# Four buffers take their places in SBUF ahead of the 3456-byte buffer, in a one-core fp32 block of attention and Mish MLP

## The chip, the cores and the metric

The kernel runs on one core of one Trainium2 chip. The metric is the device time of one execution in microseconds; lower is better. Three runs of the kernel before took 1113.59, 1114.18 and 1112.23 us, the median is 1113.59 us. A further execution was recorded by the profiler and took 1110.76 us.

## What is computed

The reference takes x of 2048 tokens by 576 features, normalises it, and adds two branches to it:

```python
def reference(A_x, A_wqkv, A_wo, B_x, B_w1, B_b1, B_w2):
    x = A_x
    xn = _layernorm(x, axis=-1)
    return x + _A_ref(xn, A_wqkv, A_wo) + _B_ref(xn, B_w1, B_b1, B_w2)

def _A_ref(x, wqkv, wo):         # 32 heads of 18; each token sees 8 tokens, 2 apart, backwards
    ...
    logits = jnp.einsum("bhsd,bhswd->bhsw", q, kg) * scale
    logits = jnp.where(mask[None, None, :, :], logits, -1e9)
    attn = _softmax(logits, axis=-1)
    o = jnp.einsum("bhsw,bhswd->bhsd", attn, vg)
    return (lambda x, *d: x.transpose(*d))(o, 0, 2, 1, 3).reshape(B, S, D) @ wo

def _B_ref(x, w1, b1, w2):       # 576 -> 4608 -> 576
    h = jnp.einsum("bsd,df->bsf", x, w1) + b1
    sp = jnp.log1p(jnp.exp(-jnp.abs(h))) + jnp.where(h > 0, h, jnp.zeros_like(h))
    act = h * jnp.tanh(sp)
    return jnp.einsum("bsf,fd->bsd", act, w2)
```

## The kernel before

**Numbers.** Every matrix product runs on TensorE in a rounded fp32 type. To keep fp32 accuracy each operand is split into a high and a low part, and three products (high by high, high by low, low by high) are summed in PSUM. A weight tile therefore holds two halves: `t[:, 0]` is the high part (a ScalarE copy, line 365) and `t[:, 1]` the low part (a VectorE subtraction, line 366).

**Tiling.** The tokens go in two halves `hf` of 1024, each in two blocks `b` of 512 tokens. The transposed, normalised input of a block is the tile `xt` (one for each block, `X0` and `X1` in the code); sums of the two blocks are the tiles `S`. The 4608 hidden features go in 18 pairs `q` of 128-column blocks. The products of the MLP are done with seven products of half blocks where eight would be usual, so the weights of a pair appear in four tiles: `wa` (the first weight block as it is, 640 columns), `wc` (a part of the second, 384 columns) and `t0`, `t1` (differences, 512 columns each).

**The first product** of the MLP is `m1_part` (lines 892 to 925). For each `hf` and `q` it runs six parts. `prod` (line 830) issues six matmuls, each with a 128x128 piece of a weight tile held in TensorE and 512 columns of `xt` or `S` streamed past it; `rest` (line 838) issues two more for the last 64 features. Part 0 is 14 matmuls with `wa` against `X0` (12 from line 834, 2 from line 840), and part 4 ends with 2 matmuls with `wa` against `X1` (line 840). So `wa` is the held weight in 16 matmuls of each of the 36 steps. All the other parts hold pieces of `t0`, `t1` or `wc`.

**The second product** (`m2_pair` line 927, `m2_cols` line 1042, `p_item` line 1016) holds a piece of an activation tile (`act` or `u`) and streams 288 columns of the second weight.

**Order.** The instructions stand in an order written by hand: a list `plan` of steps, to which the code attaches small functions (loads, splits, attention steps) by tables of offsets. Each engine executes its own list in that order and waits on semaphores where it needs another engine. SyncE's queue carries every load and store. Attention runs beside the products: GpSimd multiplies (lines 697 and 736), VectorE reduces (702, 742), VectorE transposes the result `og` of a pair of heads groups into `oT` (line 762), and four or more stores write `oT` to DRAM (line 771).

**Places in SBUF.** Tiles are requested from one pool by a tag. A tag gets its place the first time that it is requested, behind the places given before, and all later tiles of the tag use it again. The last ones to be given are these, in bytes from the start of a partition, as the built program has them:

| tile (tag) | first byte before | size |
|---|---|---|
| 3456-byte buffer (`r3`) | 206,400 | 3456 |
| `wa` of even q (`wa1`) | 209,856 | 5120 |
| `q`, two buffers | 214,976 and 216,128 | 1152 each |
| `wa` of odd q (`wa0`) | 217,280 | 5120 |
| `L`, two buffers | 222,400 and 223,424 | 1024 each |
| `m`, two buffers | 224,448 and 224,576 | 128 each |
| `og` | 224,704 | 2304 |
| `oT` | 227,008 | 2304 |

The 3456-byte buffer is requested first by `za_high` (line 515) for a weight tile of the query, key and value projection, by way of the table `YHOME` (line 495, `"T2": ("r3", "a0")`). It serves later as a place for other weights and for one raw activation. All other weight and input tiles lie below it: `wq`, `t0`, `t1` at 60,224, 64,320 and 68,416; `xt` of the two blocks at 85,312 and 161,344; `wc` at 103,744 and 107,328; the second weights at 110,912 to 124,736; activations at 140,864 to 157,248; `S` at 181,824, 190,016 and 198,208.

Of the kernel before, what the change touches and what calls it, by code (L numbers as in the profile page):

```python
# [9 lines left out]
F32 = mybir.dt.float32  # L10
F32R = mybir.dt.float32r
# [7 lines left out]
P = 128  # L19
# [4 lines left out]
TJ = SH // P  # L24
# [6 lines left out]
PU = 2  # L31
CU = 2 * DH
# [98 lines left out]
def block_kernel(ctx: ExitStack, tc: tile.TileContext, x, wq, wo, w1, b1, w2, mask, out):  # L131
# [4 lines left out]
    sb = ctx.enter_context(tc.tile_pool(name="sb", bufs=2))  # L136
# [97 lines left out]
    def newton1():  # L234
        newton(rs1, ve1, y1, nc.gpsimd)
        nc.gpsimd.tensor_mul(nm1, mv1[:, :, 0:1], rs1)
        nc.gpsimd.tensor_scalar(nm1, nm1, -1.0, None, op0=ALU.mult)
# [74 lines left out]
    def home(kind, i):  # L312
        if kind == "wq":
            g, k = divmod(i, 5)
            tag, bufs = (("wb", 3) if k < 3 else ("wc", 2)) if g % 2 == 0 else (("a0", 3) if k < 3 else ("a1", 2))
            return tag, bufs, 432
        if kind == "wa":
            return f"wa{(i + 1) % 2}", 1, 5 * P
        if kind == "wc":
            return "wc", 2, 3 * P  # L320
        if kind == "w2":
            return "w2", 4, D
        return "wb", 3, 4 * P

    def new(kind, hf, i):
        tag, bufs, width = home(kind, i)
        if tag == "wc":
            return sb.tile([P, 7 * P], F32R, tag=tag, bufs=bufs, name=f"{kind}_{hf}_{i}")[:, 0:2 * width].rearrange(
                "p (h c) -> p h c", h=2)
        return sb.tile([P, 2, width], F32R, tag=tag, bufs=bufs, name=f"{kind}_{hf}_{i}")  # L330
# [183 lines left out]

    def za_high(name, k=0):
        tag = YHOME[name][k]
        t = yw[name, k] = sb.tile([P, 2, 432], F32R, tag=tag, bufs=BUFS[tag], name=f"yw_{name}_{k}")
        nc.scalar.copy(t[:, 0], zraw[name, k])

# [128 lines left out]
    def load_kv(hf, i, part):  # L648
        g, u = divmod(i, UQ)
        t = sb.tile([P, TJ + HALO, CU], F32, tag="kv", bufs=4, name=f"kv{part}_{hf}_{i}")  # L650
        src = kv_d[g][part * UQ + u, hf * SH, 0:1]
        nc.sync.dma_start(
            t.rearrange("p t c -> p (t c)"),
            bass.AP(tensor=src.tensor, offset=src.offset, ap=[[TJ * CU, P], [1, (TJ + HALO) * CU]]))
        return t
# [9 lines left out]
    def win(kv, c0, cn, j0, jn):  # L665
        base = kv[:, j0, c0:c0 + 1]
        return bass.AP(tensor=base.tensor, offset=base.offset,
                       ap=[list(base.ap[0]), [CU, jn], [DIL * CU, W], [1, cn]])
# [5 lines left out]
    def attention(hf):  # L674
# [4 lines left out]
        def flush(all_=False):  # L679
            for n in list(waiting):  # L680
                if all_ or (hf, n) not in SUMS:
                    waiting.pop(n)()

        sums[hf] = waiting
        for pair in range(NQ * UQ // PU):
            n = f"{hf}_{pair}"
            vs, nxt = [], []
            L = sb.tile([P, PU, TJ, W, 2], F32, tag="L", bufs=2, name=f"L_{n}")
            hj = TJ // 2
            for k, (kt, q) in enumerate(kqs):  # L690
                for c in range(2):
                    flush()
                    pr = sb.tile([P, hj, W, CU], F32, tag="pr", bufs=2, name=f"pr_{n}_{k}_{c}")
                    j0 = c * hj
                    hh = hj // 2
                    for x in range(0, hj, hh):
                        nc.gpsimd.tensor_tensor(  # L697
                            out=pr[:, x:x + hh], in0=q[:, j0 + x:j0 + x + hh, None, :].to_broadcast([P, hh, W, CU]),
                            in1=win(kt, 0, CU, j0 + x, hh), op=ALU.mult)

                    def red(pr=pr, k=k, j0=j0, L=L):
                        nc.vector.tensor_reduce(  # L702
                            L[:, k, j0:j0 + hj].rearrange("p j w h -> p (j w h)"),
                            pr.rearrange("p j w (h d) -> p (j w h) d", h=2), axis=AX, op=ALU.add)
                    waiting[next(step)] = red
                    if k == 0:
                        vs.append(load_kv(hf, pair * PU + c, 1))
                    yield
            flush(True)
            next(step)  # L710
            if hf == 0:
                lm = L[0:2].rearrange("p k j w h -> p k (j w h)")
                nc.vector.tensor_add(lm, lm, mk[:, None, :].to_broadcast([2, PU, TJ * W * 2]))
            m = sb.tile([P, PU * TJ, 2], F32, tag="m", bufs=2, name=f"m_{n}")
            Lf = L.rearrange("p k j w h -> p (k j) w h")
            Lt = Lf.rearrange("p j w h -> p j h w")
            nc.vector.tensor_reduce(m, Lt, axis=AX, op=ALU.max)
            mb = m[:, :, None, :].to_broadcast([P, PU * TJ, W, 2])
            nc.vector.tensor_sub(Lf, Lf, mb)
            Ls = L.rearrange("p k j w h -> p (k j w h)")  # L720
            if (hf, pair) == (0, 4):
                soon.append(lambda: nc.scalar.preload_act_table_set("natural_log_exp_and_others"))
            soon.append(lambda Ls=Ls: nc.scalar.activation(Ls, Ls, AF.Exp, scale=SCALE))
            if (hf, pair) == (0, 4):
                soon.append(root1)
            yield
            nc.vector.tensor_reduce(m, Lt, axis=AX, op=ALU.add)
            nc.vector.reciprocal(m, m)
            nc.vector.tensor_mul(Lf, Lf, mb)  # L729
            og = sb.tile([P, PU * CU, TJ], F32, tag="og", bufs=1, name=f"og_{n}")  # L730
            for k, vt in enumerate(vs):
                for h in range(2):
                    flush()
                    pr = sb.tile([P, TJ, DH, W], F32, tag="pr", bufs=2, name=f"pv_{n}_{k}_{h}")
                    for x in range(0, TJ, hj):
                        nc.gpsimd.tensor_tensor(  # L736
                            out=pr[:, x:x + hj].rearrange("p j d w -> p j w d"),
                            in0=L[:, k, x:x + hj, :, h:h + 1].to_broadcast([P, hj, W, DH]),
                            in1=win(vt, h * DH, DH, x, hj), op=ALU.mult)

                    def red(pr=pr, og=og, c0=k * CU + h * DH, last=(k, h) == (PU - 1, 1), pair=pair):
                        nc.vector.tensor_reduce(og[:, c0:c0 + DH, :].rearrange("p d j -> p j d"), pr, axis=AX,  # L742
                                                op=ALU.add)
                        if last:
                            turn = lambda: o_turn(hf, pair, og)
                            if now[0] == at["z", 0, 1]:
                                plan[now[0] + 1][0].append(turn)
                            else:
                                soon.append(turn)
                    waiting[next(step)] = red  # L750
                    if (hf, pair, k, h) == (0, *(4, 0, 1)):
                        newton1()
                    if k == 0 and (pair + 1) * PU + h < NQ * UQ:
                        nxt.append(load_kq(hf, (pair + 1) * PU + h))
                    yield
            kqs = nxt
# [1 line left out]
        yield  # L758

    def o_turn(hf, pair, og):  # L760
        oT = sb.tile([P, PU * CU * TJ], F32, tag="oT", bufs=1, name=f"oT_{hf}_{pair}")
        nc.vector.transpose(oT, og.rearrange("p c j -> p (c j)"))
        soon.append(lambda: o_send(hf, pair, oT))

# [771 lines left out]
    def spot(hf, q, i):  # L1536
        return at["s", hf, q, i]

    for q in range(NP):
        if q == 0:  # L1540
            i = z0 + 8
            ps_ = dict(raw=i - 3, sums=i + 1, wa=i, wc=i + 3, t0=i + 2, t1=i + 3)
        elif q == 1:
            i = z0 + 10
# [16 lines left out]
    for q in range(1, 2 * OC + 1):  # L1561
        i = spot(0, q, (3,2)[q > 1])
# [5 lines left out]
    i = spot(0, NP - 1, 0)  # L1568
# [5 lines left out]
    i = at["q", 1, 0, 1, 1]  # L1574
# [4 lines left out]
    for q in range(NP):  # L1579
        if q == 0:  # L1580
            i = at["z", JB - 1, 0]
            ps_ = dict(wa=i - 7, t0=i - 6, t1=i - 5, wc=i - 4)
        elif q == 1:
            i = spot(1, 0, 0)
# [39 lines left out]
    i = at["q", 1, 0, 1, 1]  # L1624
# [9 lines left out]
    for n in range(0, JB, 2):  # L1634
        i = at["q", 0, 1, 0, n]
# [4 lines left out]
    for n in range(TJ):  # L1640
        i = spot(0, 2 + n, 2)
# [3 lines left out]
    i = spot(0, NP - 2, 6)  # L1645
# [7 lines left out]
    for n, (name, pr) in enumerate((name, pr) for name in ("P4", "P5", "P2", "P3") for pr in range(2)):  # L1653
        i = items[dict(P4=0, P5=2, P3=2, P2=3)[name]][2] + pr
# [26 lines left out]
    for n in range(steps - len(last_steps)):  # L1681
# [4 lines left out]
    early = {0: (8,), 1: (0, 2, 4, 6, 8), 2: (0, 4, 7), 3: (0, 2, 4, 6), 4: (0, 2, 4, 7), 5: (0, 2, 4, 6), 6: (0, 2, 4, 7),  # L1686
             7: (0, 2, 4, 6), 8: (0, 2, 4, 7), 9: (0, 2, 4, 6), 10: (0, 2, 4, 7), 11: (0, 2, 4, 6), 12: (1, 4, 8), 13: (1, 3, 7)}
# [17 lines left out]
    i = spot(1, 2 * OC + 2, 0)  # L1705
# [11 lines left out]
    i = spot(1, NP - 1, 0)  # L1717
# [71 lines left out]
```

## Time and profile before

| | |
|---|---|
| median of three runs | 1113.59 us |
| profiled execution | 1110.76 us |
| its span, first to last instruction | 1109.0 us |
| TensorE matmuls (PE) busy | 1094.4 us, 6478 instructions |
| VectorE (DVE) busy | 874.6 us |
| GpSimd (POOL) busy | 780.1 us |
| ScalarE (ACT) busy | 508.7 us |
| mean granted TensorE clock | 0.998 |

PE is the matrix unit, PEld its loading of the held weights, which overlaps the matmul before. SPq is SyncE's queue. In a row such as "L834 PE MATMUL h<-xt,wa" the first name is what is written, the names behind the arrow are what is read, with buffer numbers left out, so `t` stands for `t0` and `t1`, `w` for the second weights. "Mean ns of one" of a matmul counts from its start to its modelled end, which overlaps the start of the next; the distance from one start to the next is what a matmul costs.

### The profile page before, as it was taken

The page shows a single profiled execution, that of the slowest core. Times are in us where ns is not written, and L with a number is a line of the kernel's source. Part 1 is how long each engine was busy: PE and PEld are TensorE (multiplying, and loading weights), DVE is VectorE, ACT ScalarE, POOL GpSimd, SP SyncE. Part 2 cuts the span into 40 slices and gives each one's busy share as a digit, 9 for nine tenths or more (in the row PEclk, how much of TensorE's full clock was granted, in tenths as well). Part 3 has the DMA queues.
Part 4 walks back from the last instruction along what each step waited for, and adds up shares of the span by engine and source line. Part 5 has one row for each costly group of instructions (what it writes and reads, how often), then busy time and mean ns, then how long its engine had stood idle before and what let it go on. Part 6 is the DMA issues. An engine that isn't in the chain of part 4 may idle for free.

```text
span 1109.0 us, 18148 instructions
## 1 busy us (share of the span) xinstructions
PE 1094.4 (99%) x6478; PEld 1005.4 (91%) x6478; DVE 874.6 (79%) x1433; ACT 508.7 (46%) x935; POOL 780.1 (70%) x635
## 2 busy tenths in 40 slices
PE   8999999999999999999999999999999999989998
PEld 8998899999999999999998889989999989989998
DVE  6775888898987888987756568887888895787786
ACT  5554554454456444454333354444444434243353
POOL 2434967878776776867679669778676799967442
PEclk9999999999999999999999999999999999999999
DMA  6769997867877586666598899675668476487864
GB/s 225 271 232 344 358 327 247 273 241 265 273 250 249 209 280 220 232 251 203 186 303 276 272 339 337 239 237 200 212 216 266 167 241 219 152 292 243 252 218 141
DMA packets 183006, 276.01 MB, mean 249 GB/s; under 512 B 53346, under 2 KB 124292, under 8 KB 182916
## 3 DMA queue, kind: packets, MB, share of 16 engines
q1 hardware_dynamic: 182916, 274.86, 73.4%
q8 instruction: 51, 0.84, 0.3%
q14 instruction: 39, 0.32, 0.1%
HBM read 162.16 MB, written 112.66 MB: 248 GB/s over the span
## 4 chain that ended last, share of the span: by engine, by line
PE 92%; DMA 2%; DVE 2%; issue 1%; POOL 1%; SPq 1%; ACT 0%; DVEq 0%; ACTq 0%; POOLq 0%
PE h L834 29%; PE po L936 21%; PE po L1028 12%; PE pq L459 7%; PE po L1049 6%; PE h L840 6%; PE o L1232 5%; PE z L607 4%; PE y L559 1%; PE yT L559 1%; PE yB L559 1%; DMA pw<-kept_T 1%; DMA kept_yB<-yw_B 1%; DMA w<-kept_w 1%; PE ta L166 0%
## 5 line engine op out<-in xcount | busy, mean ns | idle before, releaser
L936 PEld LDWEIGHTS po<-w,act 128*128 128x128 f32 x1728 | 236.5, 188 | 5.7
L936 PE MATMUL po<-w,act 128*128 128x288 f32 x1728 | 240.6, 295 | 0.0
L697 POOL TENSOR_TENSOR pr<-q,kv 128x576 f32<-128x576 f32 x128 | 195.6, 1553 | 10.2 <-DMA q<-q_d 4.6
L736 POOL TENSOR_TENSOR pv<-L,kv 128x576 f32<-128x576 f32 x128 | 176.5, 1477 | 31.6 <-DVE L L729 14.5
L886 POOL TENSOR_TENSOR act<-c,act 128x512 fp32r<-128x512 f32 x69 | 93.7, 1358 | 99.6 <-ACT act L885 94.1
L1028 PEld LDWEIGHTS po<-pw,u 128*128 128x128 f32 x1008 | 138.3, 188 | 5.5 <-issue 1.9
L1028 PE MATMUL po<-pw,u 128*128 128x288 f32 x1008 | 140.7, 295 | 1.5 <-DMA pw<-kept_T 1.5
L940 DVE TENSOR_TENSOR acc<-po,acc 128x288 f32<-128x288 f32 x288 | 118.5, 449 | 23.1 <-PE po L936 21.8
L834 PE MATMUL h<-xt,t 128*128 128x512 f32 x432 | 111.3, 392 | 2.1 <-ACT t L365 1.5
L834 PE MATMUL h<-S,t 128*128 128x512 f32 x432 | 110.4, 391 | 0.1
L834 PE MATMUL h<-xt,wa 128*128 128x512 f32 x432 | 106.2, 395 | 0.0
L880 ACT ACTIVATE c<-c,b1c 128x512 f32<-128x512 f32 x69 | 50.0, 725 | 121.5 <-DVE c L879 121.3
L742 DVE TENSOR_REDUCE og<-pv 128x144 f32<-128x1152 f32 x64 | 86.0, 1345 | 19.4 <-POOL pv L736 19.3
L702 DVE TENSOR_REDUCE L<-pr 128x64 f32<-128x1152 f32 x64 | 85.9, 1342 | 17.6 <-POOL pr L697 17.5
L834 PEld LDWEIGHTS h<-xt,wa 128*128 128x128 f32 x432 | 81.3, 189 | 18.5
L834 PEld LDWEIGHTS h<-xt,t 128*128 128x128 f32 x432 | 79.0, 188 | 18.1 <-ACT t L365 1.9
L459 PE MATMUL pq<-wq,xt 128*128 128x432 f32 x448 | 91.8, 362 | 0.8 <-ACT xt L172 0.7
L834 PEld LDWEIGHTS h<-S,t 128*128 128x128 f32 x432 | 78.0, 188 | 13.4 <-ACT rm L868 0.5
L459 PEld LDWEIGHTS pq<-wq,xt 128*128 128x128 f32 x448 | 83.0, 188 | 5.6 <-ACT xt L172 1.1
L1049 PEld LDWEIGHTS po<-w,act 128*128 128x128 f32 x576 | 79.9, 191 | 5.0 <-DVE accP L1052 3.4
L1049 PE MATMUL po<-w,act 128*128 128x288 f32 x576 | 81.2, 298 | 2.9 <-DVE accP L1052 2.9
L868 ACT COPY c<-h 128x512 f32<-128x512 f32 x69 | 40.4, 585 | 86.5 <-PE h L840 43.5
(259 smaller groups left out, 1989.2 us busy)
## 6 DMA issues: line engine op xcount, KB each, us to landing
kv<-kv_d SPq DMA_DIRECT2D x64, 396.0 KB, 6.1
kept_t<-t SPq DMA_DIRECT2D x36, 512.0 KB, 4.1
t<-kept_t SPq DMA_DIRECT2D x36, 512.0 KB, 4.6
pw<-kept_T SPq DMA_DIRECT2D x24, 576.0 KB, 6.1
rw<-in_w SPq DMA_DIRECT2D x36, 320.0 KB, 5.0
kept_wa<-wa SPq DMA_DIRECT2D x18, 640.0 KB, 4.6
wa<-kept_wa SPq DMA_DIRECT2D x18, 640.0 KB, 5.2
rw<-in_w SPq DMA_DIRECT2D x36, 288.0 KB, 5.7
```

The lines of the kernel that those rows point to most:

```text
L459: nc.tensor.matmul(pq[:, 0:432], XT[:, xi, tok], wt[wi][:, hl, 0:432], start=i == 0, stop=i == len(seq) - 1)
L697: nc.gpsimd.tensor_tensor(out=pr[:, x:x + hh], in0=q[:, j0 + x:j0 + x + hh, None, :].to_broadcast([P, hh, W, CU]), in1=win(kt, 0, CU, j0 + ...
L702: nc.vector.tensor_reduce(L[:, k, j0:j0 + hj].rearrange("p j w h -> p (j w h)"), pr.rearrange("p j w (h d) -> p (j w h) d", h=2), axis=AX, ...
L736: nc.gpsimd.tensor_tensor(out=pr[:, x:x + hj].rearrange("p j d w -> p j w d"), in0=L[:, k, x:x + hj, :, h:h + 1].to_broadcast([P, hj, W, DH]),
L742: nc.vector.tensor_reduce(og[:, c0:c0 + DH, :].rearrange("p d j -> p j d"), pr, axis=AX, op=ALU.add)
L834: nc.tensor.matmul(ph, wt[:, wl, wk * P:(wk + 1) * P], X[:, xs, :], start=first and i == 0, stop=last and i == len(seq) - 1, skip_group_ch ...
L840: nc.tensor.matmul(ph, wt[:, wl, off * P:(off + 1) * P], X[:, xs, :], start=False, stop=wl == 1, skip_group_check=True)
L886: nc.gpsimd.tensor_tensor(out=a[:, 1, :], in0=t, in1=a[:, 0, :].bitcast(F32), op=ALU.subtract)
L936: nc.tensor.matmul(po, acts[hf, q, b, j][:, al, tok], done["w2", hf, 2 * q + j][:, wl, c * HC:(c + 1) * HC], start=i == 0, stop=i == 5)
L940: nc.vector.tensor_tensor(out=t, in0=po, in1=t, op=ALU.add)
L1028: nc.tensor.matmul(po, units[e, k, qq][:, al, tok], w[:, qq, wl, :], start=i == 0, stop=i == 5)
L1049: nc.tensor.matmul(po, acts[hf, q, b, j][:, al, tok], done["w2", hf, 2 * q + j][:, wl, c * HC:(c + 1) * HC], start=i == 0, stop=i == 5)
```

## The change

Just before the 3456-byte buffer is requested for the first time, four tiles are requested: `wa` for q = 0 and q = 1, the first `og` and the first `oT`. They are kept in a dictionary, and the code that would request them later takes them from there. (The dictionary's name `early` is given once more, further down in the same function, to a table of plan steps with whole numbers as keys; the four entries then stand in that table, and nothing else reads them.) No computation, transfer or order is touched: in the built programs every engine has the same instructions in the same order with the same semaphore waits as before, and only the addresses of these tiles differ:

| tile | first byte before | first byte after | remainder by 256, before | after |
|---|---|---|---|---|
| `wa` of even q | 209,856 | 206,400 | 192 | 64 |
| `wa` of odd q | 217,280 | 211,520 | 192 | 64 |
| `og` | 224,704 | 216,640 | 192 | 64 |
| `oT` | 227,008 | 218,944 | 192 | 64 |
| 3456-byte buffer | 206,400 | 221,248 | 64 | 64 |
| `q` | 214,976 and 216,128 | 224,704 and 225,856 | 192 and 64 | 192 and 64 |
| `L` | 222,400 and 223,424 | 227,008 and 228,032 | 192 and 192 | 192 and 192 |
| `m` | 224,448 and 224,576 | 229,056 and 229,184 | 192 and 64 | 192 and 64 |

One weight tile of the output projection (`wo_r`) lives in the place of `wa` of odd q and moves with it. All other tiles stay where they were.

```diff
+    early = {}
+
+    def reserve():
+        for i in range(2):
+            early[f"wa{(i + 1) % 2}"] = sb.tile([P, 2, 5 * P], F32R, tag=f"wa{(i + 1) % 2}", bufs=1, name=f"wa_0_{i}")
+        early["og"] = sb.tile([P, PU * CU, TJ], F32, tag="og", bufs=1, name="og_0")
+        early["oT"] = sb.tile([P, PU * CU * TJ], F32, tag="oT", bufs=1, name="oT_0_0")
+
     def new(kind, hf, i):
         tag, bufs, width = home(kind, i)
+        if tag in early:
+            return early.pop(tag)
...
     def za_high(name, k=0):
         tag = YHOME[name][k]
+        if tag == "r3":
+            reserve()
...
-            og = sb.tile([P, PU * CU, TJ], F32, tag="og", bufs=1, name=f"og_{n}")
+            og = early.pop("og") if "og" in early else sb.tile([P, PU * CU, TJ], F32, tag="og", bufs=1, name=f"og_{n}")
...
-        oT = sb.tile([P, PU * CU * TJ], F32, tag="oT", bufs=1, name=f"oT_{hf}_{pair}")
+        oT = early.pop("oT") if "oT" in early else sb.tile(
+            [P, PU * CU * TJ], F32, tag="oT", bufs=1, name=f"oT_{hf}_{pair}")
```

## The prediction

> **What bounds the kernel now.** I read the page first: which engine is busy, and who makes up the chain that ended last.
>
> ```profile
> PE 1094.4 (99%) x6478; PEld 1005.4 (91%) x6478; DVE 874.6 (79%) x1433; ACT 508.7 (46%) x935; POOL 780.1 (70%) x635
> PE 92%; DMA 2%; DVE 2%; issue 1%; POOL 1%; SPq 1%; ACT 0%; DVEq 0%; ACTq 0%; POOLq 0%
> ```
>
> TensorE is busy 1094.4 of 1109.0 us and holds 92% of the chain. With instructions, order and waits unchanged, the time can move in two ways only: some instruction takes another time because its operands lie elsewhere, or the engines meet differently. So the view to read next is the one by tile, for how long one matmul takes with each weight that it holds: `wa`, which moves, then `t` and `wc`, which stay.
>
> ```profile
> L834 PE MATMUL h<-xt,wa x432: 389/393/405, 94.7 to 1017.2; 128*128 128x512 f32 x144
> L840 PE MATMUL h<-xt,wa x144: 389/396/405, 97.5 to 1030.4; 128*128 128x512 f32 x144
> L834 PE MATMUL h<-S,t x432: 387/389/497, 98.0 to 1024.9; 128*128 128x512 f32 x144
> L834 PE MATMUL h<-xt,t x432: 387/389/504, 99.3 to 1029.9; 128*128 128x512 f32 x144
> L834 PE MATMUL h<-S,wc x216: 387/390/496, 105.6 to 1035.0; 128*128 128x512 f32 x108
> L840 PE MATMUL h<-xt,wc x144: 389/389/398, 102.1 to 1035.5; 128*128 128x512 f32 x144
> ```
>
> The three numbers are shortest, median and longest in ns. The shape is the same in all six rows, and so is the work. `t` and `wc`, in five buffers from 60,224 to 107,328, sit at 389 or 390; `wa` alone is above them, at 393 on line 834 and 396 on line 840. These durations run over the start of the next matmul, so I check the difference in a timeline, from one start to the next, in a quiet stretch of the first half:
>
> ```profile
> 300.68 0.64 PE L840 MATMUL h<-xt,wa 128*128 128x512 f32 x2
> 301.16 3.35 PE L936 MATMUL po<-w,act 128*128 128x288 f32 x24
> 304.35 1.53 PE L834 MATMUL h<-S,wc 128*128 128x512 f32 x6
> 305.72 0.62 PE L840 MATMUL h<-xt,wc 128*128 128x512 f32 x2
> 306.18 2.95 PE L834 MATMUL h<-xt,wa 128*128 128x512 f32 x12
> 308.97 0.62 PE L840 MATMUL h<-xt,wa 128*128 128x512 f32 x2
> 309.42 1.52 PE L834 MATMUL h<-xt,t 128*128 128x512 f32 x6
> 310.78 3.34 PE L936 MATMUL po<-w,act 128*128 128x288 f32 x24
> ```
>
> The 12 with `wa` last from 306.18 to 308.97, 2.79 us or 232.5 ns each; the 6 with `t` from 309.42 to 310.78, 1.36 us or 226.7 each. The pair on `X1` with `wa` takes 0.48 us (300.68 to 301.16), the pair on `X1` with `wc` 0.46 us (305.72 to 306.18). No wait stands in these rows, so these nanoseconds are TensorE's own, and TensorE is the chain here. What sets `wa` apart is where it lies: its two buffers are the only held weights of the large products that start 192 bytes past a multiple of 256; `t`, `wc`, activations, `xt` and `S` all start at 64. After the change `wa` starts at 64 too.
>
> **The change part by part.**
>
> *The `wa` matmuls* (432 on line 834, 144 on line 840, together 36 steps of 16). What they lose if they become like the rest, three ways. By the medians above: 4 ns x 432 + 7 ns x 144 = 2.7 us. By the timeline: a step's 16 take 2.79 + 0.45 + 0.48 = 3.72 us; 16 at 226.7 ns take 3.63, so 0.09 us a step and 3.3 us in 36. By the means of the grouped view:
>
> ```profile
> L834 PE MATMUL h<-xt,t 128*128 128x512 f32 x432 | 111.3, 392 | 2.1 <-ACT t L365 1.5 <-DVE t L366 0.7
> L834 PE MATMUL h<-xt,wa 128*128 128x512 f32 x432 | 106.2, 395 | 0.0
> L840 PE MATMUL h<-xt,wa 128*128 128x512 f32 x144 | 45.5, 397 | 0.0
> L840 PE MATMUL h<-xt,wc 128*128 128x512 f32 x144 | 44.6, 391 | 0.0
> ```
>
> there it is 3 ns x 432 + 6 ns x 144 = 2.2 us, with some long matmuls mixed into the mean of `t`. So 2.2 to 3.3 us; I take 3.0, between the median and the timeline, since a start-to-start distance is the nearest to a cost. All of it lies on the path. What could be lost again in TensorE's later waits is seen in the view of waits:
>
> ```profile
> PE po L1049 <- DVE accP L1052: 2.9, 1, 2.9
> PE po L1028 <- DMA pw<-kept_T: 1.5, 1, 1.5
> PE h L834 <- ACT t L365: 1.5, 1, 1.5
> 114.19 0.74 PE L834 MATMUL h<-xt,t 128*128 128x512 f32 x2 [1.47 <-ACT t L365]
> 891.80 0.27 PE po L1028 x3
> 892.07 6.09 DMA pw<-kept_T
> ```
>
> The wait for `t` falls at 114.19 us, with two of 36 steps' `wa` begun. The transfer `pw` starts, in the chain, as TensorE leaves line 1028, so it comes earlier with TensorE. The wait for `accP` is a rival below.
>
> The Trainium skill (SBUF — State Buffer, section "Who interferes with whom") speaks against this term: it lets only VectorE and GpSimd get in each other's way and says that PE and ACT "never wait on anyone"; by that the address of a weight costs nothing and the sum is 0 us. The rows above differ by 4 to 7 ns in 576 matmuls, which it doesn't provide for, so I give it a rival's chance and no more.
>
> *The streamed side.* `wo_r`, in the place of `wa` of odd q, is streamed, not held:
>
> ```profile
> L1232 PE MATMUL o<-wo_r,ob x48: 288/295/307, 1053.2 to 1105.6; 128*128 128x288 f32 x48
> L1049 PE MATMUL po<-w,act x576: 288/295/442, 918.9 to 1051.4; 128*128 128x288 f32 x192
> ```
>
> Its median is that of the second weights, 295 ns: 0 us, at most some 48 x 1 ns.
>
> *`og`, `oT` and the transfers.* `q`, `L`, `m` and the 3456-byte buffer keep their remainder by 256. `og` and `oT` go from 192 to 64; VectorE writes them; SyncE's queue moves `wa`:
>
> ```profile
> L742 DVE TENSOR_REDUCE og<-pv 128x144 f32<-128x1152 f32 x64 | 86.0, 1345 | 19.4 <-POOL pv L736 19.3
> L702 DVE TENSOR_REDUCE L<-pr 128x64 f32<-128x1152 f32 x64 | 85.9, 1342 | 17.6 <-POOL pr L697 17.5
> kept_wa<-wa SPq DMA_DIRECT2D x18, 640.0 KB, 4.6
> wa<-kept_wa SPq DMA_DIRECT2D x18, 640.0 KB, 5.2
> ```
>
> The reduction into `og` takes as long as that into `L`, which is in another place, so an address is not seen in it; bounded by that 3 ns, 64 of them are 0.2 us, on an engine that idles over 19 us before them. Whatever a transfer of `wa` gains or loses, the `wa` matmuls have an idle time of 0.0 in the grouped rows above, so no one waits for it; if that cover went, 36 transfers a few per cent off 5 us would be some 0.2 us each. I take 0 for both, 0.5 us either way for the range.
>
> *Sum.* Profiled execution 1110.76 us (span 1109.0 and 1.76 around it), less 3.0: 1107.8. The median of the three runs lies 2.8 us above that execution, and I carry the difference over: 1113.59 - 3.0 = **1110.6 us**, 0.27% faster.
>
> **The rivals.**
>
> *The address by 256 is not the cause.* `wa` differs from `t` in two more things: it lies above 206,400 before and after, and line 834 pairs it with `X0` alone. If the upper region is slow for held weights, nothing changes: 1113.6. If `X0` as the streamed side is slow, only the 72 matmuls against `X1` gain, 7 to 13 ns each or under 1 us: 1112.8. For it: no other held weight lies up there. Against it: the pair on `X1`, where `wc` and `wa` stream the same tile, shows the gap too; and both `wa` buffers, 7424 bytes apart, share one row with a shortest of 389 and a longest of 405, which a border of regions between them would have pulled apart. The skill's rule above ends here as well.
>
> *Another collision of VectorE with GpSimd (the slower side).* One place in the profile shows what a shifted meeting can cost:
>
> ```profile
> 963.25 2.79 POOL L697 TENSOR_TENSOR pr<-q,kv 128x576 f32<-128x576 f32 x2
> 963.33 8.01 DVE L1133 TENSOR_TENSOR raw_T<-raw_T,woh_T 128x576 fp32r<-128x576 f32 x2
> 966.02 1.28 POOL L886 TENSOR_TENSOR act<-mn,act 128x512 fp32r<-128x512 f32 x1
> 967.26 2.79 POOL L697 TENSOR_TENSOR pr<-q,kv 128x576 f32<-128x576 f32 x2
> ...
> 973.62 4.97 PE L1049 MATMUL po<-w,act 128*128 128x288 f32 x24 [2.95 <-DVE accP L1052]
> 978.43 1.55 PE L834 MATMUL h<-S,t 128*128 128x512 f32 x6
> L1133 DVE TENSOR_TENSOR raw_T<-raw_T,woh_T x4: 744/940/7344, 963.3 to 985.3; 128x576 fp32r<-128x576 f32 x4
> ```
>
> A VectorE subtraction that can take 744 ns takes 7344 while GpSimd works without a break from 963.25 to 970.05. Behind it on VectorE wait an add for ScalarE (`c`, line 879) and the adds `accP` that free PSUM, and for these TensorE: 2.95 us idle, and the next 24 matmuls last 4.81 us to the next row's start, where 24 of this shape from 310.78 on have a row of 3.34, not 4.97. One such catch costs 2.95 + 1.6 us, some 4.6 us. A TensorE that is up to 3 us earlier meets GpSimd at other points. One catch more gives 1110.6 + 4.6 = 1115.2, about the old time; two give 1119.8. It decides for slower once new stalls pass 3.0 + 2.2 = 5.2 us. For it: GpSimd has no gap in these rows. Against it: its work hangs on TensorE's results, so most of the meeting moves along as a whole. The skill names this mechanism (SBUF — State Buffer, "Who interferes with whom": a VectorE instruction with two SBUF inputs and a GpSimd instruction that reads SBUF take turns, the later one blocked); the trace agrees, with 7344 against 744 ns.
>
> *The same catch goes away.* By the same argument the present one may be missed: 1110.6 - 4.6 = 1106.0.
>
> That the change doesn't do what it says is out: the addresses in the built program are those of the table above.
>
> **How the numbers follow.** About 0.2% (2.2 us, so 1111.4 and 1115.8) is what a measurement of this kernel can tell from no change. The forecast has a chance of 0.52, with its own range 1109.5 to 1111.8 (2.2 to 3.3 us, half a microsecond for the transfers and half for the spread of a median); 0.42 of it is below 1111.4, 0.10 above, as the gain is only a little over the bound. That the cause is another: 0.15, of which 0.13 within the bound and 0.02 below. The catch more: 0.20, of which 0.05 (one) is about the old time and 0.15 slower. The catch gone: 0.13, all faster. Faster 0.57, same 0.28, slower 0.15. The range takes the forecast, the first rival, the case of one catch and the catch gone: 1106.0 to 1115.5, which leaves out 0.15.
>
> **What would show it.** Right: the rows of `wa` in the view by tile fall to 389 or 390 ns on both lines, the 12 matmuls with `wa` take 2.72 us from start to start and the pair on `X1` 0.46, while the rows of `t` and `wc` stay at 389; TensorE's busy time falls by about 3 us; the reductions stay at 1345 ns and the transfers at about 5 us. If the rows of `wa` stay at 393 and 396, the first rival holds; if only the row of line 840 falls, it is `X0`. If the rows fall and the time does not, the idle times of TensorE have grown, and the rows of line 1133 and the waits for `accP` or for a ScalarE split will say where. Wrong altogether would be a row of some other tile that becomes slower, such as weights streamed out of the moved 3456-byte buffer.

## The result, and the profile after

| | before | after |
|---|---|---|
| median of 16 runs | 1112.59 us | 1107.59 us |
| lowest and highest | 1110.55, 1114.18 us | 1104.68, 1112.36 us |
| profiled execution | 1110.76 us | 1104.68 us |
| its span and granted clock | 1109.0 us, 0.998 | 1102.9 us, 1.000 |

The ratio is 0.9962, with an interval of 0.9951 to 0.9974: 4.2 us less, between 2.9 and 5.5. It compares the means of the 16 runs, 1112.58 and 1108.37 us; the medians lie 5.0 us apart. The kernel became faster. The profiled execution after the change is the fastest of its 16.

The page of the changed kernel, its lines on how busy the engines are and on who makes up the chain of work that ended last:

```profile
PE 1088.4 (99%) x6478; PEld 1002.3 (91%) x6478; DVE 872.4 (79%) x1433; ACT 508.6 (46%) x935; POOL 781.1 (71%) x635
PE 94%; DMA 2%; DVE 2%; issue 1%; SPq 1%; ACT 0%; POOL 0%; DVEq 0%; POOLq 0%; ACTq 0%
```

TensorE is busy 1088.4 us where it was 1094.4, and still 99% of the span. It holds 94% of the chain, where it held 92%. Of the difference in span, 6.1 us, 6.0 are found in TensorE's busy time; VectorE's changes by 2.2 us, ScalarE's and GpSimd's by 1.0 or less.

The view by tile (shortest, median and longest duration in ns; lines 834 and 840 of before are now 847 and 853):

```profile
L847 PE MATMUL h<-xt,wa x432: 387/389/401, 95.2 to 1011.2; 128*128 128x512 f32 x144
L853 PE MATMUL h<-xt,wa x144: 388/389/397, 97.9 to 1024.3; 128*128 128x512 f32 x144
L847 PE MATMUL h<-S,t x432: 387/389/500, 98.4 to 1018.9; 128*128 128x512 f32 x144
L847 PE MATMUL h<-xt,t x432: 387/389/502, 99.8 to 1023.9; 128*128 128x512 f32 x144
L847 PE MATMUL h<-S,wc x216: 387/389/504, 106.0 to 1028.9; 128*128 128x512 f32 x108
L853 PE MATMUL h<-xt,wc x144: 389/389/397, 102.5 to 1029.3; 128*128 128x512 f32 x144
```

The first two rows are what the change moved: `wa` fell from 393 and 396 to 389 and 389, and its longest from 405 to 401 and 397. The rows of `t` did not move; the median of `S` with `wc` went from 390 to 389. All six tiles now read alike.

The timeline of TensorE in the stretch that the prediction showed, some 0.7 us earlier in the span (start, duration, engine and line; a row's end runs over the next row's start, so a cost is a distance between two starts):

```profile
300.02 0.62 PE L853 MATMUL h<-xt,wa 128*128 128x512 f32 x2
300.47 3.34 PE L949 MATMUL po<-w,act 128*128 128x288 f32 x24
303.65 1.53 PE L847 MATMUL h<-S,wc 128*128 128x512 f32 x6
305.02 0.62 PE L853 MATMUL h<-xt,wc 128*128 128x512 f32 x2
305.47 2.88 PE L847 MATMUL h<-xt,wa 128*128 128x512 f32 x12
308.19 0.61 PE L853 MATMUL h<-xt,wa 128*128 128x512 f32 x2
308.64 1.52 PE L847 MATMUL h<-xt,t 128*128 128x512 f32 x6
310.00 2.27 PE L949 MATMUL po<-w,act 128*128 128x288 f32 x16
```

The 12 with `wa` take 305.47 to 308.19, 2.72 us (they took 2.79); the pair on `X1` with `wa` takes 300.02 to 300.47, 0.45 us (it took 0.48). The pair with `wc` has 0.45 us and the 6 with `t` 1.36 us, where they had 0.46 and 1.36.

What stands beside the path, first VectorE's reductions and the streamed `wo_r` in the grouped view (busy us, mean ns, idle time ahead), then the transfers (median us to landing):

```profile
L754 DVE TENSOR_REDUCE og<-pv 128x144 f32<-128x1152 f32 x64 | 86.0, 1345 | 21.0 <-POOL pv L748 20.8
L714 DVE TENSOR_REDUCE L<-pr 128x64 f32<-128x1152 f32 x64 | 85.9, 1343 | 18.3 <-POOL pr L709 18.2
L1245 PE MATMUL o<-wo_r,ob 128*128 128x288 f32 x48 | 10.3, 295 | 0.0
```

```profile
kept_wa<-wa SPq DMA_DIRECT2D x18, 640.0 KB, 4.9
wa<-kept_wa SPq DMA_DIRECT2D x18, 640.0 KB, 5.1
```

The reductions and `wo_r` are what they were, 1345 and 1343 ns and 295 ns. The transfers take 4.9 and 5.1 us against 4.6 and 5.2; that is no matter of the address, as the run `e3_behind` below, with `wa` at 192, has 4.9 and 5.1 too.

The view of waits for TensorE (us in total, times, longest), and the catch of VectorE against GpSimd in a timeline of all engines:

```profile
PE po L1062 <- DVE accP L1065: 3.3, 1, 3.3
PE h L847 <- ACT t L375: 1.6, 1, 1.6
PE po L1041 <- DMA pw<-kept_T: 1.2, 1, 1.2
```

```profile
958.95 2.94 POOL L709 TENSOR_TENSOR pr<-q,kv 128x576 f32<-128x576 f32 x2
959.17 8.01 DVE L1146 TENSOR_TENSOR raw_T<-raw_T,woh_T 128x576 fp32r<-128x576 f32 x2
962.97 2.93 POOL L709 TENSOR_TENSOR pr<-q,kv 128x576 f32<-128x576 f32 x2
969.46 3.44 PE L1062 MATMUL po<-w,act 128*128 128x288 f32 x24 [3.28 <-DVE accP L1065]
972.74 1.55 PE L847 MATMUL h<-S,t 128*128 128x512 f32 x6
```

The catch is still there, at 959 us instead of 963: VectorE's two subtractions in the row of line 1146 take 8.01 us beside GpSimd's products of line 709, and TensorE then waits 3.28 us for `accP`. One thing differs: the 24 matmuls behind the wait have a row of 3.44 us here, where they had 4.97. The granted clock tells the two apart: its mean over 973 to 980 us was 0.76 in the profile before, and over 969 to 976 us it is 1.00 here. Behind this wait, which lasts 2.9 to 3.3 us in all ten profiles of this document, the granted clock stands at one half for 3.41 us in seven of them, for 6.83 us in two and not at all in this one.

**All matmuls, from start to start.** For the account, each matmul's start was subtracted from the next one's, with the held weight, the streamed operand and their addresses taken from the built program (574 of the 576 `wa` matmuls and 65 of the 70 that run just before a `wa` matmul and hold another tile could be used; intervals over 300 ns, which hold waits, are left out). Mean ns for 512 columns, and of the second products (288 columns) and the 432-column ones:

```
                        held wa   t or wc, next   t or wc,   432 col   288 col
                                  held is wa      others
before                  232.9     232.5           228.2      197.8     133.4
changed kernel          226.9     226.9           227.9      197.8     132.9
e1_wa_only              226.9     226.8           227.9      197.9     133.5
e2_out_only             233.0     232.8           228.2      197.9     133.4
e3_behind               233.0     232.5           228.2      197.8     133.4
e4_shift128             226.8     227.0           227.8      197.9     133.3
e5_t192                 227.2     229.1           231.3      197.6     133.6
e6_x192                 232.0     226.8           228.4      197.5     133.3
e7_wa128                233.1     226.1           228.7      198.2     133.4
```

In sums: `wa` itself went from 133.71 to 130.22 us, 3.49 us less; the matmuls that run just before a `wa` piece is held went from 15.11 to 14.74, 0.37 us less. Together 3.9 us. The profiled pair lies 2.2 us further apart; 1.5 of it is the row behind the wait for `accP` (4.97 against 3.44). That row changes from one execution to the next and not with the address, as the same place in the profile of the first experiment, which has the new address of `wa` too, shows (it is also why the 288-column mean is 132.9 in the changed kernel's row of the table and 133.3 to 133.6 elsewhere):

```profile
971.38 6.13 PE L1060 MATMUL po<-w,act 128*128 128x288 f32 x24 [3.22 <-DVE accP L1063]
```

### The profile page after: what moved, and what is told of

Its sections match the earlier page's. It is cut to its first block, busy times and chain, and to the rows that moved or that the text cites. A ratio compares the mean times of both kernels' runs of the same rounds, so it can differ in the third digit from the quotient of the medians.

```text
span 1102.9 us, 18148 instructions
## 1 busy us (share of the span) xinstructions
PE 1088.4 (99%) x6478; PEld 1002.3 (91%) x6478; DVE 872.4 (79%) x1433; ACT 508.6 (46%) x935; POOL 781.1 (71%) x635
## 4 chain that ended last, share of the span: by engine, by line
PE 94%; DMA 2%; DVE 2%; issue 1%; SPq 1%; ACT 0%; POOL 0%; DVEq 0%; POOLq 0%; ACTq 0%
PE h L847 29%; PE po L949 21%; PE po L1041 12%; PE pq L469 7%; PE po L1062 7%; PE h L853 6%; PE o L1245 5%; PE z L619 3%; PE y L571 1%; PE yT L571 1%; PE yB L571 1%; DMA pw<-kept_T 1%; DMA kept_yB<-yw_B 0%; DMA acc<-in_x 0%; DMA z_T<-kept_yT 0%
## 5 line engine op out<-in xcount | busy, mean ns | idle before, releaser
L847 PE MATMUL h<-xt,wa 128*128 128x512 f32 x432 | 103.9, 389 | 0.0
L754 DVE TENSOR_REDUCE og<-pv 128x144 f32<-128x1152 f32 x64 | 86.0, 1345 | 21.0 <-POOL pv L748 20.8
L714 DVE TENSOR_REDUCE L<-pr 128x64 f32<-128x1152 f32 x64 | 85.9, 1343 | 18.3 <-POOL pr L709 18.2
```

Of the source, the lines that this page charges most:

```text
L714: nc.vector.tensor_reduce(L[:, k, j0:j0 + hj].rearrange("p j w h -> p (j w h)"), pr.rearrange("p j w (h d) -> p (j w h) d", h=2), axis=AX, ...
L847: nc.tensor.matmul(ph, wt[:, wl, wk * P:(wk + 1) * P], X[:, xs, :], start=first and i == 0, stop=last and i == len(seq) - 1, skip_group_ch ...
```

## The experiments

Each starts from the changed kernel. In the first seven, no instruction, order or wait differs from it; only addresses do. The kernel before was run again beside them: a median of 1113.33 us (35 runs) beside the first four and 1112.37 (35 runs) beside the last four, on another chip. So experiments are best compared by their ratios to before.

**Which of the moved tiles it is: `wa` alone.**

```diff
-        early["og"] = sb.tile([P, PU * CU, TJ], F32, tag="og", bufs=1, name="og_0")
-        early["oT"] = sb.tile([P, PU * CU * TJ], F32, tag="oT", bufs=1, name="oT_0_0")
```

> Only the two buffers of wa go ahead of the 3456-byte buffer (to 206,400 and 211,520, 64 past a multiple of 256); og and oT keep their old places (224,704 and 227,008). If the held weight's address is the cause: rows of wa at 389 ns on both lines, ratio to before 0.996 as with the whole change. If og and oT bring the gain: rows of wa may fall, ratio 1.000.

Measured: 1107.71 us, ratio 0.9955 (0.9938 to 0.9971). Its view by tile (lines 845 and 851 here):

```profile
L845 PE MATMUL h<-xt,wa x432: 387/389/401, 95.1 to 1015.9; 128*128 128x512 f32 x144
L851 PE MATMUL h<-xt,wa x144: 388/389/398, 97.8 to 1029.1; 128*128 128x512 f32 x144
```

`wa` at a remainder of 64, `og` and `oT` in their old places: the whole gain is there.

**The other half: `og` and `oT` alone.**

```diff
-        for i in range(2):
-            early[f"wa{(i + 1) % 2}"] = sb.tile([P, 2, 5 * P], F32R, tag=f"wa{(i + 1) % 2}", bufs=1, name=f"wa_0_{i}")
```

> Only og and oT go ahead (206,400 and 208,704, both 64 past); wa stays at 192 past, but at other places than before (214,464 and 221,888). If the held weight's address by 256 is the cause: rows of wa stay at 393 and 396 ns, ratio 1.000. If og and oT bring the gain: ratio 0.996.

Measured: 1111.88 us, ratio 0.9996 (0.9981 to 1.0012). The same two rows by tile:

```profile
L845 PE MATMUL h<-xt,wa x432: 387/392/404, 95.0 to 1017.1; 128*128 128x512 f32 x144
L851 PE MATMUL h<-xt,wa x144: 389/396/404, 97.8 to 1030.3; 128*128 128x512 f32 x144
```

Nothing is gained, and `wa` (at 192) keeps its slow rows.

**The same tiles requested early, but behind the 3456-byte buffer.**

```diff
+        t = yw[name, k] = sb.tile([P, 2, 432], F32R, tag=tag, bufs=BUFS[tag], name=f"yw_{name}_{k}")
         if tag == "r3":
             reserve()
-        t = yw[name, k] = sb.tile([P, 2, 432], F32R, tag=tag, bufs=BUFS[tag], name=f"yw_{name}_{k}")
```

> The same four buffers are reserved together, but right behind the 3456-byte buffer: wa at 209,856 and 214,976, again 192 past a multiple of 256, og and oT at 192 past too. If the remainder by 256 is the cause: rows of wa at 393 and 396 ns, ratio 1.000. If reserving them early, or a lower place, is the cause: ratio near 0.996 and wa at 389.

Measured: 1112.68 us, ratio 1.0006 (0.9990 to 1.0023). By tile (lines 847 and 853 again):

```profile
L847 PE MATMUL h<-xt,wa x432: 390/392/404, 95.5 to 1021.2; 128*128 128x512 f32 x144
L853 PE MATMUL h<-xt,wa x144: 389/396/404, 98.2 to 1034.4; 128*128 128x512 f32 x144
```

Here `wa` of even q starts at 209,856, below the fast 211,520 of the changed kernel, and of odd q at 214,976. So neither the region nor the early request decides; the remainder does, or something that goes with it.

**Is it the remainder itself? All tiles 128 bytes later.** A 128-byte tile that nothing uses is put ahead of all of them (and 512 of the 1024 bytes that the program sets aside for dynamic transfers are given up, to make room). Every weight, activation and input that started at 64 now starts at 192, `wa` too.

```diff
+    const.tile([P, 32], F32, name="pad")
     zeros = sb.tile([2 * UQ, HALO * CU], F32, tag="pr", bufs=2, name="zeros")
...
-    nc = _bacc.Bacc("TRN2", target_bir_lowering=False, num_devices=1, dynamic_dma_scratch_size=1024)
+    nc = _bacc.Bacc("TRN2", target_bir_lowering=False, num_devices=1, dynamic_dma_scratch_size=512)
```

> The changed kernel with an unused 128-byte buffer ahead of all tiles, room for which comes from a smaller scratch area: all held and streamed tiles go from 64 to 192 past a multiple of 256. If a held weight at 192 is slow by itself: all 512-column matmuls rise to 393 ns and more (1656 times about 5 ns, at least 8 us), the 432- and 288-column ones perhaps too; ratio to before 1.003 or more. If only the difference between held and streamed remainders counts: wa, t and wc all at 389, ratio 0.996.

Measured: 1108.31 us, ratio 0.9967 (0.9951 to 0.9983). By tile, `wa` and, for the other weights, `t`:

```profile
L847 PE MATMUL h<-xt,wa x432: 387/389/398, 94.7 to 1014.3; 128*128 128x512 f32 x144
L853 PE MATMUL h<-xt,wa x144: 388/389/393, 97.4 to 1027.5; 128*128 128x512 f32 x144
L847 PE MATMUL h<-xt,t x432: 388/389/501, 99.2 to 1027.1; 128*128 128x512 f32 x144
```

This is the run that corrects the prediction. 192 is not slow: held weights at 192 stay at 389 when what streams past them is at 192 too. What `wa` had in the kernel before was a distance of 128, by 256, from the streamed `xt`.

**Another weight at a distance: `t`.** 128 unused bytes ahead of the three buffers of `t` and 128 behind them (and again the 512 bytes given up, as in the next two).

```diff
     def first_cast(k, eng):
+        if k == 0:
+            sb.tile([P, 32], F32, tag="pad0", bufs=1, name="pad0")
         t = done["wq", 0, k] = new("wq", 0, k)
+        if k == 0:
+            sb.tile([P, 32], F32, tag="pad1", bufs=1, name="pad1")
```

> The changed kernel with one more displacement: the three buffers that hold `t` (864 of the large matmuls) start 128 bytes later than all the rest, that is 192 past a multiple of 256 while the streamed `xt` and `S` stay at 64; `wa` stays at 64. Theory (a held weight and a streamed operand 128 bytes apart by 256 cost time, whichever weight it is): the rows of `t` rise from 389 to 392 to 396, the row of `wa` stays at 389; 864 x 5 to 6 ns is 4.3 to 5.2 us more than the changed kernel's 1107.6, so 1111.9 to 1112.8, about the time of before. Rival (it is something about `wa` alone, its region, its producer or its transfers): `t` stays at 389 and the time at 1107.6.

Measured: 1110.00 us, ratio 0.9991 (0.9975 to 1.0007). By tile, `wa` and both rows of `t`:

```profile
L847 PE MATMUL h<-xt,wa x432: 389/389/395, 94.7 to 1019.2; 128*128 128x512 f32 x144
L847 PE MATMUL h<-S,t x432: 387/393/628, 97.9 to 1027.0; 128*128 128x512 f32 x144
L847 PE MATMUL h<-xt,t x432: 387/393/498, 99.3 to 1032.0; 128*128 128x512 f32 x144
```

`t` becomes slow, 389 to 393 in the median, and `wa` stays at 389: it is no property of `wa`. From start to start the matmuls that hold `t` take 232.4 ns in place of 227.8, 4.0 us for all 864. The time came out 2 us below the forecast; the ratio's interval, 2.8 us below before to 0.8 above, reaches it. At the same granted clock, 0.998, five runs have a median of 1109.89 us, 1.1 below that of 17 runs of before, where the starts would make the two about equal; this difference stays open.

**The streamed side at a distance: `X0`.** Now every weight stays at 64.

```diff
+            if (hf, b) == (0, 0):
+                sb.tile([P, 32], F32, tag="pad0", bufs=1, name="pad0")
             XTs[hf, b] = sb.tile([P, 9 + b, TB], F32R, tag=f"xt{b}", bufs=1, name=f"xt_{hf}_{b}")
+            if (hf, b) == (0, 0):
+                sb.tile([P, 32], F32, tag="pad1", bufs=1, name="pad1")
```

> The changed kernel with the streamed side displaced: only `X0` of `xt` starts 192 past a multiple of 256; all held weights, `wa` too, stay at 64. Theory (only the difference counts): the row of `wa` on line 849 or so (432 matmuls, all against `X0`) is back at 393; half of the row of the remainder products (those against `X0`) is slow again and its longest again over 400; `t` and `wc` against `X1` stay at 389. 504 x 6 ns is 3.0 us, and the 432-column products that hold `X0` may add up to 1 us: 1110.6 to 1111.6. Rival (the start of the held weight decides, and the run with everything moved by 128 was fast for another reason): `wa` stays at 389, 1107.6.

Measured: 1108.68 us, ratio 0.9973 (0.9954 to 0.9992). By tile (the lines are 851 and 857 here):

```profile
L851 PE MATMUL h<-xt,wa x432: 387/393/404, 94.8 to 1017.8; 128*128 128x512 f32 x144
L857 PE MATMUL h<-xt,wa x144: 388/392/404, 97.5 to 1031.0; 128*128 128x512 f32 x144
L857 PE MATMUL h<-xt,wc x144: 389/389/397, 102.1 to 1036.0; 128*128 128x512 f32 x144
```

`wa` keeps its remainder of 64 (it lies 256 bytes lower) and is slow again, 393 and 392, because `X0` moved; its remainder products are half against `X0` and half against `X1`, and their row has a median between the two. `wc` against `X1` stays at 389. That settles the mechanism from the other side: from start to start the matmuls of `wa` against `X0` took 226.9 and 226.8 ns with both at 64 and with both at 192, 232.1 with `wa` at 192 and `X0` at 64, and 232.7 with `wa` at 64 and `X0` at 192. The rows are as forecast; the time, forecast at 1110.6 to 1111.6, is 1.9 us below that, and its interval spans 1107.3 to 1111.5 on the median of before beside it, so it tells neither for nor against the size. The 432-column products that hold `X0` cost nothing (197.5 ns in the table above).

**A distance of 64 in place of 128: `wa` at 128.**

```diff
     def reserve():
+        sb.tile([P, 16], F32, tag="pad0", bufs=1, name="pad0")
         for i in range(2):
             early[f"wa{(i + 1) % 2}"] = sb.tile([P, 2, 5 * P], F32R, tag=f"wa{(i + 1) % 2}", bufs=1, name=f"wa_0_{i}")
+        sb.tile([P, 48], F32, tag="pad1", bufs=1, name="pad1")
```

> The changed kernel with `wa` alone 64 bytes later: 128 past a multiple of 256, the rest at 64, so held and streamed operand are 64 bytes apart. It asks for the shape of the cost. If the cost is one of 128 bytes alone (two operands in opposite halves of 256 bytes): rows at 389, 1107.6. If any difference by 256 costs the same: rows at 393 and 396, 1111.6. If the cost grows with the distance: rows at about 391 and 392, 1109.6.

Measured: 1112.12 us, ratio 0.9996 (0.9979 to 1.0014): the gain is gone. By tile (lines 849 and 855):

```profile
L849 PE MATMUL h<-xt,wa x432: 388/398/398, 95.2 to 1019.3; 128*128 128x512 f32 x144
L855 PE MATMUL h<-xt,wa x144: 390/394/398, 98.0 to 1032.6; 128*128 128x512 f32 x144
L855 PE MATMUL h<-xt,wc x144: 388/389/397, 102.5 to 1037.6; 128*128 128x512 f32 x144
```

398 and 394: a distance of 64, here with the weight ahead, costs as much as one of 128, 233.1 ns from start to start against 232.9. Two details differ. The last matmul before a held `wa` takes 226.1 ns here and took 232.5 before the change. And `t` against `X1`, which did not move in its relation, took 229.7 ns in this profile against 227.7; why is open.

**A version that should beat both: the second weights cut at 1024 bytes.** In the first half of the tokens the second product takes 576 columns of `w` as 288 and 288, and the second piece starts 1152 bytes in, at a distance of 128 by 256 from the held activation.

```diff
-            for c in range(2):
-                po = ps.tile([P, 512], F32, tag="out", bufs=4, name=f"po_{hf}_{q}_{b}_{jj}_{c}")[:, 0:HC]
+            for c, (lo, hi) in enumerate(((0, 256), (256, 576))):
+                po = ps.tile([P, 512], F32, tag="out", bufs=4, name=f"po_{hf}_{q}_{b}_{jj}_{c}")[:, 0:hi - lo]
...
-                                     done["w2", hf, 2 * q + j][:, wl, c * HC:(c + 1) * HC],
+                                     done["w2", hf, 2 * q + j][:, wl, lo:hi],
...
-                t = accs[hf][b * JB + jj][:, c * HC:(c + 1) * HC]
+                t = accs[hf][b * JB + jj][:, lo:hi]
```

> The changed kernel with another cut of the second weights in the first half: the 576 columns that line 949 takes as 288 and 288 are taken as 256 and 320, so that the second piece starts 1024 and not 1152 bytes in, no longer 128 bytes apart from the held activation by 256. The same work, the same number of instructions. Theory: the 864 matmuls of the second piece, 133.1 instead of 131.2 ns from start to start before, lose 1.9 ns each: 1.6 us, so 1106.0, if the time of a matmul goes with its columns otherwise. Rival (the 1.9 ns come from the second bank of the output or from the columns' end): 1107.6, and up to 1 us more if narrower matmuls hide their weight load worse.

Measured: 1109.84 us, ratio 0.9973 (0.9959 to 0.9987) to before; no better than the changed kernel. The grouped view with shapes kept apart (busy us, mean ns):

```profile
L949 PE MATMUL po<-w,act 128*128 128x320 f32 x864 | 150.5, 309 | 0.0
L949 PE MATMUL po<-w,act 128*128 128x256 f32 x864 | 126.5, 282 | 0.0
L847 PE MATMUL h<-xt,wa 128*128 128x512 f32 x432 | 103.9, 389 | 0.0
```

From start to start, all six matmuls of each sum, with the changed kernel beside it:

```
first piece    256 columns 119.3 ns    (288 columns, no distance:     131.6)
second piece   320 columns 147.1 ns    (288 columns, distance of 128: 133.5)
both                       266.4 ns    (265.1)
```

(The expectation's 131.2 and 133.1 are of the first five of each six, without intervals over 180 ns.) The pair of pieces costs 1.3 ns more, where 1.9 less was forecast; over 864 pairs that is 1.1 us, and by the ratios the run lies 1.2 us above the changed kernel, with intervals that overlap. So time does not simply follow the columns: 32 fewer columns save 12.3 ns, 32 more cost 13.6.

That the 1.9 ns between the two pieces of 288 are the price of the distance is not shown. In the run with everything moved by 128 the second piece, now streamed at 64, is again both the distant and the slow one (131.7 and 133.5). The pieces trade places in the output projection (line 1245, `wo` against `oa`, which lies in a place of `t` and moves with it): 132.5 and 133.0 ns in the changed kernel, 133.8 and 132.8 in the run that moved `t`, 48 matmuls each. There the distance costs 0.5 to 1.0 ns; the rest is open.

No version tried is clearly faster than the changed kernel: moving `wa` alone has a ratio of 0.9955 and moving everything 0.9967, both within its interval.

## Why the prediction was right, and where it was not

*The term of the sum was the right one.* `wa`'s rows fell to 389 on both lines, the 12 matmuls to 2.72 us and the pair on `X1` to 0.45, the values that the prediction named; moving `wa` alone gave all of it, and moving `og` and `oT` alone none.

*Its size was too small.* The term was 3.0 us, of a range of 2.2 to 3.3. From start to start it measured 3.49 us for `wa` itself, 6.07 ns for each matmul (5.2 against `X0`, 12.3 against `X1`): the timeline's own 3.3 was near, and the medians of durations, which say 2.7 and pulled the choice down to 3.0, were not: durations run over the next start. Beside it 0.37 us lie in matmuls that hold `t` or `wc` while the next piece is `wa` (232.5 to 226.9 ns), which the sum did not have at all. Together 3.9 us; the measured 4.2 us (2.9 to 5.5) agree with it. Among runs with the same granted clock, 0.998, the medians are 1110.95 and 1111.59 before (17 and 10 runs, beside the last four and the first four experiments) and 1107.5 after (9 runs): 3.5 to 4.1 us.

*The time was covered in part by luck.* 1107.59 us lies in the whole range, 1106.0 to 1115.5, but below the forecast's own, 1109.5 to 1111.8. The whole range went so far down only for a catch that goes away, and the catch stayed.

*The starting point was 1.0 us too high.* The three runs had a median of 1113.59, the 16 runs 1112.59. From there the term of 3.0 gives 1109.6, and a term of 3.9 gives 1108.7. The rest to 1107.59 lies within the spread of the runs.

*The cause was put too narrowly.* The prediction's step was that `wa` is slow because it starts 192 past a multiple of 256. With everything at 192 it is fast; with `t` at 192 and the rest at 64, `t` is slow; with `X0` at 192 and `wa` at 64, `wa` is slow; with `wa` at 128, it is slow. What counts in all of these is whether the held weight and the operand that streams past it start at the same remainder by 256. (Distances of 64 and 128 were tried. A distance of 256 is free: in the changed kernel `wa` is an odd number of 256 bytes from `X0` and an even number from `X1`, and takes 226.9 ns against both.) For this change the two statements give the same number, so the time could not tell them apart.

*The Trainium skill* (SBUF — State Buffer, section "Who interferes with whom") says that PE and ACT "never wait on anyone". It speaks there of engines that share ports, not of start addresses; read as widely as the prediction read it, every one of these runs should have had `wa` and `t` at 389. The runs have 392 to 398 wherever the two remainders differ; the measurement decides.

*The rivals.* That the region above 206,400 is slow fell with the third experiment, and that `X0` is slow as the streamed side fell with the row of line 847. One catch of VectorE more, or one fewer, did not happen in the profiled execution: the shortest and the longest of `raw_T` read as they did (744 and 7344 ns before), and TensorE waits once for `accP`, as before. The prediction's price of a catch, 4.6 us, held 1.6 us for the slower row behind the wait; the same catch came without it here, at a granted clock of 1.00, so that part goes with the clock and not with each catch:

```profile
L1146 DVE TENSOR_TENSOR raw_T<-raw_T,woh_T x4: 745/1266/7340, 959.2 to 980.1; 128x576 fp32r<-128x576 f32 x4
```

*What was costed at nothing* stayed at nothing: the reductions into `og` at 1345 ns, `wo_r` at 295, the transfers of `wa` at 4.9 and 5.1 us with an idle time of 0.0 behind them, and the two waits for `t` and `pw` at 1.6 and 1.2 us (1.5 and 1.5 before).

Left open: whether a matmul is slowed as its own weight or as the next one is read. At a distance of 128 the matmul before the first distant weight is slow too (232.5 ns), at a distance of 64 it isn't (226.1). In the run that moved `X0` it is fast (226.8) although the `wa` matmuls behind it are slow: it streams `X1`, which has the remainder of the coming `wa`. So at 128 the coming weight counts, against the operand that streams at that moment; the held weight's own part is not told apart from it.

## What to carry to other kernels

When the same matmul shape reads a few nanoseconds apart in the view by tile, look at where both operands start, and compare the held one's remainder by 256 bytes with the streamed one's; here 4 to 7 ns on 389 were worth 0.4% of the whole kernel. Such a cause is told from its look-alikes by three cheap layouts, each with the same instructions: move everything, move another held tile, move the streamed tile. And take the size of a small term from start-to-start distances over all its instances, the matmuls just before them included, not from one quiet stretch.

## What the runs showed of the hardware that was not expected

- A held weight and a streamed operand at different remainders by 256 cost about 6 ns on a 512-column matmul (226.9 to 233 ns from start to start; 12 ns in the pair of `wa` on `X1`), 64 bytes apart as much as 128 apart; common remainders of 64 and of 192 are equally fast (226.9 and 226.8). On 432 columns with `X0` held nothing is seen (197.5 against 197.8); on 288 columns it is 0.5 to 1.0 ns where the two pieces trade places.
- 256, 288 and 320 columns take 119.3, 131.6 and 147.1 ns, all at a common remainder: the steps of 32 columns are 12.3 and 15.5 ns, so two pieces of 288, though one is at a distance (265.1 ns), were no dearer than 256 and 320 (266.4).
- After the same wait of about 3 us, the next 24 matmuls have a row of 3.44, 4.97 or 6.13 us in different executions, with the granted clock at one half for none, 3.41 or 6.83 us of it and the work behind it. That spread alone is more than half of what this change is worth.
